# Gated linear attention and two expert layers on one core: prologue reordered, passes outermost, GpSimd's two-input steps on VectorE

## The chip, the cores and the metric

The kernel runs on one core of one Trainium2 chip. The metric is device microseconds (us) of one execution, the median of three runs. The engines are named as in the profile: PE is TensorE's matmuls and PEld its weight loads, DVE is VectorE, ACT is ScalarE, POOL is GpSimd, SP is SyncE, which issues most of the DMAs here.

## What is computed

Three parts follow each other; the output of each is the input of the next.

```python
f = 1 / (1 + exp(-f_logit))                      # attention: 4 batches, 8 heads, 768 steps, head size 48
for t in range(S):
    state = f[t][:, None] * state + outer(k[t], v[t])
    y[t] = q[t] @ state
x = y as [3072, 384]
p = domain_probs / (domain_probs.sum(-1) + 1e-9)  # mixture: 4 experts, 384 -> 1024 -> 384
x = sum over e of p[:, e] * (max(x @ w1[e], 0) @ w2[e])
out = ((x @ u1) * (x @ u2)) @ u3 @ uo             # last layer: 384 -> 1024 -> 1024 -> 384
```

All arrays are float32; the last layer's weights u1, u2, u3 and uo arrive as 64-bit floats.

## The kernel before, in words

**Precision.** The large products run in a form in which an operand is split into a high half (a copy rounded to the matmul's type, `fp32r`, by ScalarE) and a low half (the original minus the high half). Each product is three matmuls, or passes: high by high, high by low, low by high. `PASSES` (line 22) lists them as pairs (weight half, hidden half).

**Attention** goes in 24 chunks of 128 steps. Each chunk m is a list of steps: `a_exp`, `a_add`, `a_scan` (the running product of the gates, line 242), `a_ln`, `a_rec` (its reciprocal), `a_k` (keys times the running product, line 259), `a_t` (line 265), `a_q1` and `a_q2` (queries, lines 272 and 277), `a_p` (products of keys and queries on PE, the mask on DVE), `a_st` and `a_y` (the output, PE), `a_s` (the state, line 403), then `a_xh` and `a_xl` or `a_x` and `a_d`, which split the output into the halves of x. After each block of four chunks `attn_n` (line 427) sums x, for a check of range at the end.

**The mixture** (units of kind "E") goes in three super-blocks of two blocks of 512 tokens. A block of one expert is eight units f, one for each 128 hidden columns. The first block of the first expert is cut in two of 256 tokens, so its units are half as long. A unit has two parts. `stage1` (line 706): nine matmuls into one PSUM bank, then ACT writes the high half of the hidden tile with a ReLU (L727) and DVE the low half (L728). `stage2` (line 740): nine matmuls into three banks y0 to y2, for the three thirds of the output; the loop over the thirds is outermost, that over the passes inside. After the eighth unit DVE multiplies each bank by the gate (L774, or L771 for the first expert) and POOL adds it to the accumulator (L775).

**The last layer** (kind "M") has eight blocks of 384 tokens and 27 matmuls of 384 columns a unit. Its weights are first decoded from 64 bits by nine small steps a job (`decode_a`, `decode_b`, lines 543 and 559: seven on DVE, then one on ACT, then the product L572 on POOL), 16 jobs for u1 and u2 and 30 for uo and u3; the 30 are split into halves (`hilo_c`, line 609, low half on POOL) and multiplied ahead (`w3_mm`).

**Weights** come in chunks of 128x768. `feed` (line 841), called at the head of each unit, loads chunks ahead and splits at most one: high half on ACT (L174), low half on POOL (L175). Ten split chunks are held; a chunk is split when the oldest one's last unit is past. There are 160.

**The order** is written by hand: every engine runs its instructions in the order in which the program issues them. A prologue list `asteps` brings the first two chunks through and begins the third; `(warm, n)` are matmuls whose result is not used, `(feed_, 1)` splits a chunk, `gate_` normalises the experts' probabilities on DVE (line 129), `gate_rows_` transposes them on PE and sends them to memory, and `load_gate` (line 146) reads them back, spread over the partitions. The later steps have due times and `spread` (line 796) lays them over the units. The loop over the units issues, for unit i:

```python
feed(i, 1)
stage1(i)
if ends: stage2(i - 1)          # the unit before closed its block
...                             # first half of the steps planned here
if i and not ends: stage2(i - 1)
...                             # second half
```

## Time and profile before

| | us |
|---|---|
| median of 3 runs | 1290.7 (1290.09 to 1291.15) |
| the profiled execution | 1291.08 |
| its span, first to last instruction | 1289.4 |
| PE busy | 1260.7 (98%) |
| DVE busy | 634.9 (49%) |
| POOL busy | 531.0 (41%) |
| ACT busy | 427.7 (33%) |

The mean granted clock of PE is 0.993 of full speed. A line such as L728 is line 728 of the kernel. In the profile an entry "A <- B" under waits says that A stood idle until B was done. In the table by stage a row gives the window in us, its length, then busy us and (x instructions) of PE, PEld, DVE, ACT and POOL, the clock that was granted to PE as a share of full speed, the share of the DMA engines and GB/s. Matmuls are pipelined, so the time of a group of nine is read from start to start.

### The profile page before, as it was taken

The numbers are of one execution on the slowest core, as the hardware profiler recorded it, in microseconds if no ns is written. First come the engines' busy times: TensorE is split into PE (matmuls) and PEld (weight loads), VectorE is DVE, ScalarE is ACT, GpSimd is POOL, SyncE is SP. The second block draws the span as 40 slices with busy tenths as digits, with TensorE's granted clock in tenths as the row PEclk, the third lists the DMA queues.
The fourth block names the chain that finished last, engine by engine and source line by source line (L and its number), as shares of the span: only waits on it lengthen the run. The fifth ranks groups of instructions, "written<-read, shape, count | busy, mean of one in ns | idle before, by whom it ended". The sixth has DMA issues, their size and how long they took to land.

```text
span 1289.4 us, 18213 instructions
## 1 busy us (share of the span) xinstructions
PE 1260.7 (98%) x6935; PEld 1092.9 (85%) x6935; DVE 634.9 (49%) x1035; ACT 427.7 (33%) x760; POOL 531.0 (41%) x413
## 2 busy tenths in 40 slices
PE   7889999999999999999999999999999999999997
PEld 7888888888878888787888778788888999999997
DVE  7654443334465546565336766756624242332422
ACT  5434233342332323232222323324223433443431
POOL 3656345553542516354352635635433222222310
PEclk8989999999999999999999999999999999999999
DMA  7644343542635434252224422414134133231301
GB/s 197 181 146 121 98 133 101 148 125 72 170 115 134 140 105 148 81 156 82 77 80 134 121 80 87 144 56 131 55 99 129 56 94 98 91 104 55 117 1 40
DMA packets 107263, 138.74 MB, mean 108 GB/s; under 512 B 9664, under 2 KB 80672, under 8 KB 107168
## 3 DMA queue, kind: packets, MB, share of 16 engines
q1 hardware_dynamic: 106400, 137.16, 35.9%
q8 instruction: 56, 0.92, 0.3%
q10 hardware_dynamic: 768, 0.34, 0.1%
q14 instruction: 39, 0.32, 0.1%
HBM read 115.39 MB, written 14.20 MB: 101 GB/s over the span
## 4 chain that ended last, share of the span: by engine, by line
PE 88%; DVE 6%; POOL 2%; issue 2%; ACT 1%; DVEq 0%; ACTq 0%; POOLq 0%
PE hps L721 43%; PE y L755 36%; PE wps L634 3%; PE ps L319 2%; PE psy L359 2%; PE psy L343 1%; PE warm L469 1%; POOL w L175 1%; POOL acc L775 1%; PE psu L369 1%; DVE hid L728 1%; DVE dexp L553 1%; DVE pi L268 1%; DVE dexp L552 1%; PE psk L311 1%
## 5 line engine op out<-in xcount | busy, mean ns | idle before, releaser
L721 PE MATMUL hps<-x,w 128*128 128x512 f32 (+2 forms) x2952 | 648.3, 367 | 1.6 <-DVE ab L735 1.3
L721 PEld LDWEIGHTS hps<-x,w 128*128 128x128 f32 x2952 | 532.3, 189 | 75.8 <-DVE ab L735 1.6
L755 PE MATMUL y<-hid,w 128*128 128x512 f32 (+1 forms) x1800 | 443.7, 390 | 11.5 <-DVE hid L728 8.3
L175 POOL TENSOR_TENSOR w<-raw,w 128x768 fp32r<-128x768 f32 x160 | 302.9, 1895 | 293.0 <-ACT w L174 258.5
L755 PEld LDWEIGHTS y<-hid,w 128*128 128x128 f32 x1800 | 327.8, 189 | 88.8 <-DVE hid L728 12.0
L728 DVE SCALAR_TENSOR_TENSOR hid<-hps,hid 128x512 fp32r<-128x512 f32 (+1 forms) x200 | 133.6, 668 | 385.7 <-ACT hid L727 385.6
L727 ACT ACTIVATE hid<-hps 128x512 fp32r<-128x512 f32 (+1 forms) x200 | 115.6, 578 | 392.6 <-PE hps L721 392.5
L174 ACT ACTIVATE w<-raw 128x768 fp32r<-128x768 f32 x160 | 133.8, 837 | 55.2 <-PE y L755 55.2
L735 DVE TENSOR_TENSOR ab<-hps,a 128x384 f32<-128x384 f32 x64 | 35.6, 557 | 164.0 <-PE hps L721 164.0
L572 POOL TENSOR_TENSOR dman<-dman,dexp 128x384 f32<-128x384 f32 (+1 forms) x46 | 46.2, 1004 | 166.5 <-ACT dman L570 142.1
L755 PE MATMUL y<-w,hid 128*128 128x384 f32 x576 | 110.7, 337 | 0.1
L775 POOL TENSOR_TENSOR acc<-acc,tmp 128x512 f32<-128x512 f32 x54 | 71.9, 1361 | 79.0 <-DVE tmp L774 79.0
L755 PEld LDWEIGHTS y<-w,hid 128*128 128x128 f32 x576 | 100.7, 188 | 0.5 <-DVE hid L737 0.4
L570 ACT ACTIVATE dman<-dman 128x384 f32<-128x384 f32 (+1 forms) x46 | 24.0, 521 | 153.8 <-DVE dman L569 149.0
L736 ACT ACTIVATE hid<-ab 128x384 fp32r<-128x384 f32 x64 | 33.7, 526 | 115.3 <-DVE ab L735 115.3
L734 ACT ACTIVATE a<-hps 128x384 f32<-128x384 f32 x64 | 31.5, 492 | 77.5 <-PE hps L721 76.8
L737 DVE TENSOR_TENSOR hid<-ab,hid 128x384 fp32r<-128x384 f32 x64 | 35.8, 559 | 37.9 <-ACT hid L736 37.9
L414 POOL TENSOR_TENSOR state<-us,pwe 112x384 f32<-112x384 f32 x20 | 17.4, 869 | 88.3 <-DVE us L413 72.6
L774 DVE TENSOR_TENSOR tmp<-y,pb 128x512 f32<-128x512 f32 x54 | 35.5, 684 | 14.7 <-POOL acc L775 14.7
L268 DVE SCALAR_TENSOR_TENSOR pi<-pi,r 112x512 f32<-112x512 f32 (+1 forms) x26 | 33.7, 1295 | 14.8 <-POOL pends L263 13.0
L634 PE MATMUL wps<-uoh,u 128*128 128x384 f32 x192 | 38.0, 339 | 1.4 <-POOL u L620 0.9
L245 DVE TENSOR_TENSOR_SCAN pi<-ft,capt 112x516 f32<-112x516 f32 (+1 forms) x26 | 35.7, 1378 | 4.2 <-ACT ft L238 3.9
(87 smaller groups left out, 829.6 us busy)
## 6 DMA issues: line engine op xcount, KB each, us to landing
raw<-in_w_dram SPq DMA_DIRECT2D x112, 384.0 KB, 4.1
raw<-in_u_dram SPq DMA_DIRECT2D x27, 384.0 KB, 3.6
vt<-in_vp_dram SPq DMA_DIRECT2D x24, 288.0 KB, 4.2
pb<-pdr SPq DMA_DIRECT2D x24, 256.0 KB, 4.7
raw<-u1d SPq DMA_DIRECT2D x16, 384.0 KB, 3.2
raw<-u2d SPq DMA_DIRECT2D x16, 384.0 KB, 3.3
raw<-wdr SPq DMA_DIRECT2D x16, 384.0 KB, 3.4
x<-yr SPq DMA_DIRECT2D x80, 72.0 KB, 2.8
```

Source lines behind the costliest of these rows:

```text
L174: nc.scalar.activation(out=w[:, 0], in_=raw, func=AF.Copy)
L175: nc.gpsimd.tensor_tensor(out=w[:, 1], in0=raw, in1=w[:, 0].bitcast(F32), op=ALU.subtract)
L245: nc.vector.tensor_tensor_scan(out=pi.rearrange("p n t -> p (n t)"), data0=gates_of(m, g).rearrange("p n t -> p (n t)"), data1=capt[:, g[0 ...
L268: nc.vector.scalar_tensor_tensor(out=pi, in0=pi, scalar=-1.0, in1=r, op0=ALU.mult, op1=ALU.mult)
L572: nc.gpsimd.tensor_tensor(out=out, in0=s, in1=t.bitcast(F32), op=ALU.mult)
L634: nc.tensor.matmul(wps[ft], lhsT=w[:, a, i * 128:(i + 1) * 128], rhs=uoh[g // (NF // 2)][:, g % (NF // 2), b], start=(g == 0 and n == 0), ...
L721: nc.tensor.matmul(ps, lhsT=w[:, wl, j, fs], rhs=x[:, xl, j, t0:t1], start=(n == 0), stop=(n == 3 * KD - 1))
L727: nc.scalar.activation(out=h[:, 0], in_=prods[0], func=AF.Relu)
L728: nc.vector.scalar_tensor_tensor(out=h[:, 1], in0=prods[0], scalar=0.0, in1=h[:, 0].bitcast(F32), op0=ALU.max, op1=ALU.subtract)
L737: nc.vector.tensor_tensor(out=h[:, 1], in0=ab, in1=h[:, 0].bitcast(F32), op=ALU.subtract)
L755: nc.tensor.matmul(yps[t], lhsT=lhsT, rhs=rhs, start=(f == f0 and n == 0), stop=(f == f1 and n == 2))
L775: nc.gpsimd.tensor_tensor(out=at_, in0=at_, in1=tmp, op=ALU.add)
```

## The change

1. All operations of two inputs that POOL did, but for the first two splits and the 8-column product of `a_q2` (L285), go to DVE: the low halves of the weight chunks, `a_k`, `a_q1`, the state in `a_s`, the decode's product, its low halves, and the accumulation after each block.
2. In `stage2` the loop over the passes becomes the outer one, in the order high-high, low weight by high hidden, high weight by low hidden. In the last unit of a block the thirds stay outermost, with the passes in the new order.
3. In the prologue chunk 1's halves of x come before chunk 2's scan; the gate follows the state; its transpose, its two DMAs and the first `load_gate` move behind the first unit.
4. The sum of x over a block is three sums of 512 columns instead of one of 1536.

```diff
@@ -87,7 +87,7 @@
     pends = const.tile([RP, NCH, NP], F32, name="pends")
     pw = const.tile([RP, 3, NP], F32, name="pw")
     pwe = const.tile([RP, 3, NP, 2], F32, name="pwe")
-    xsum = const.tile([128, NBLK], F32, name="xsum")
+    xsum = const.tile([128, NBLK * KD], F32, name="xsum")
     state = const.tile([RP, NP, 128], F32, name="state")
     ft = const.tile([RP, 2, NP, 1 + C], F32, name="ft")
     wdr = dram.tile([FF, DM], F32, name="wdr")
@@ -172,7 +172,8 @@
         raw = raw_q.pop(c)
         w = wp.tile([128, 2, 768], F32R, tag="w", name="w")
         nc.scalar.activation(out=w[:, 0], in_=raw, func=AF.Copy)
-        nc.gpsimd.tensor_tensor(out=w[:, 1], in0=raw, in1=w[:, 0].bitcast(F32), op=ALU.subtract)
+        eng = nc.vector if len(wts) >= 2 else nc.gpsimd
+        eng.tensor_tensor(out=w[:, 1], in0=raw, in1=w[:, 0].bitcast(F32), op=ALU.subtract)
         wts[key] = w
 
 
@@ -258,7 +259,7 @@
 
     def a_k(m, g=ALL):
         pi, k = part(m, "pi", None, g), kq_of(m, 0, g)
-        eng = nc.vector if m < 3 else nc.gpsimd
+        eng = nc.vector
         eng.tensor_tensor(out=k, in0=k, in1=pi[:, :, 1:], op=ALU.mult)
         nc.gpsimd.tensor_copy(out=pends[:, m, g[0]:g[1]].unsqueeze(2), in_=pi[:, :, C:])
 
@@ -271,7 +272,7 @@
 
     def a_q1(m, g=ALL):
         r, q = part(m, "r", None, g), kq_of(m, 1, g)
-        eng = nc.vector if m < 3 else nc.gpsimd
+        eng = nc.vector
         eng.tensor_tensor(out=q, in0=q, in1=r, op=ALU.mult)
 
     def a_q2(m, g=ALL):
@@ -411,7 +412,7 @@
             nc.vector.tensor_copy(out=us, in_=u2)
         else:
             nc.vector.tensor_tensor(out=us, in0=u2, in1=state_of(m), op=ALU.add)
-        nc.gpsimd.tensor_tensor(
+        nc.vector.tensor_tensor(
             out=state_of(m + 1), in0=us, in1=pwe[:, m % 3].unsqueeze(3).to_broadcast([RP, NP, 2, D]), op=ALU.mult
         )
 
@@ -425,9 +426,11 @@
             eng.dma_start(out=x[R + d0:R + d0 + r1 - r0, :, j].bitcast(F32), in_=yr[r0:r1, :, KD].bitcast(F32))
 
     def attn_n(b):
-        nc.vector.tensor_reduce(
-            out=xsum[:, b:b + 1], in_=xt[b][:, 0].bitcast(F32).rearrange("p j t -> p (j t)"), axis=AX.X, op=ALU.add
-        )
+        for j in range(KD):
+            i = b * KD + j
+            nc.vector.tensor_reduce(
+                out=xsum[:, i:i + 1], in_=xt[b][:, 0, j].bitcast(F32), axis=AX.X, op=ALU.add
+            )
 
     def attn_done(m):
         if m % CB == CB - 1:
@@ -445,11 +448,11 @@
             out=mx[0:RP, 0:1], in_=pends.rearrange("p m n -> p (m n)"), axis=AX.X, op=ALU.max
         )
         nc.vector.tensor_scalar(out=ok[0:RP, 0:1], in0=mx[0:RP, 0:1], scalar1=LIM, scalar2=None, op0=ALU.is_le)
-        ex = const.tile([128, NBLK], I32, name="ex")
+        ex = const.tile([128, NBLK * KD], I32, name="ex")
         nc.vector.tensor_scalar(
             out=ex, in0=xsum.bitcast(I32), scalar1=0x7F800000, scalar2=None, op0=ALU.bitwise_and
         )
-        fin = const.tile([128, NBLK], F32, name="fin")
+        fin = const.tile([128, NBLK * KD], F32, name="fin")
         nc.vector.tensor_scalar(out=fin, in0=ex, scalar1=float(0x72000000), scalar2=None, op0=ALU.is_lt)
         nc.vector.tensor_reduce(out=ok[:, 1:2], in_=fin, axis=AX.X, op=ALU.min)
         verdict.append(ok)
@@ -488,9 +491,9 @@
         (a_scan, 1, G0), (a_scan, 1, G1), (a_p, 0), (a_ln, 1, G0), (a_rec, 1, G0), (a_ln, 1, G1), (a_rec, 1, G1),
         (load_f, 1), (load_kq, 1), (load_v, 2), (warm, 5), (a_y, 0), (a_k, 1, G0), (a_t, 1, G0), (a_q1, 1, G0),
         (a_q2, 1, G0), (a_k, 1, G1), (a_t, 1, G1), (a_q1, 1, G1), (a_q2, 1, G1), (a_xh, 0), (a_s, 0), (warm, 5),
-        (a_p, 1), (a_st, 1), (feed_, 1), (a_xl, 0), (warm, 3), (a_y, 1), (a_exp, 2), (a_add, 2), (feed_, 1), (a_scan, 2),
-        (gate_,), (a_xh, 1), (a_xl, 1), (gate_rows_,), (a_ln, 2), (a_rec, 2), (a_s, 1), (warm, 5), (a_k, 2), (a_t, 2), (a_q1, 2),
-        (a_q2, 2), (feed_, 1),
+        (a_p, 1), (a_st, 1), (feed_, 1), (a_xl, 0), (warm, 3), (a_y, 1), (a_exp, 2), (a_add, 2),
+        (feed_, 1), (a_xh, 1), (a_xl, 1), (warm, 8), (a_scan, 2), (a_ln, 2), (a_rec, 2), (a_s, 1), (gate_,), (a_k, 2),
+        (a_t, 2), (a_q1, 2), (a_q2, 2), (feed_, 1),
     ]
 
     def ahead(m):
@@ -569,7 +572,7 @@
         nc.vector.scalar_tensor_tensor(out=s, in0=l, scalar=2.0**-24, in1=g, op0=ALU.mult, op1=ALU.add)
         nc.scalar.activation(out=s, in_=s, func=AF.Identity, scale=2.0**-20, bias=1.0)
         out = s if out is None else out
-        nc.gpsimd.tensor_tensor(out=out, in0=s, in1=t.bitcast(F32), op=ALU.mult)
+        nc.vector.tensor_tensor(out=out, in0=s, in1=t.bitcast(F32), op=ALU.mult)
         return out
 
     u1i, u2i, u3i, uoi = (u.bitcast(I32) for u in (u1, u2, u3, uo))
@@ -616,7 +619,7 @@
                 uoh.append(xp.tile([128, NF // 2, 2, DM], F32R, tag=f"x{2 + j}", name="uoh"))
             w = uoh[j][:, g]
         nc.scalar.activation(out=w[:, 0], in_=s, func=AF.Copy)
-        eng = nc.gpsimd
+        eng = nc.vector
         eng.tensor_tensor(out=w[:, 1], in0=s, in1=w[:, 0].bitcast(F32), op=ALU.subtract)
         if key[0] == "3":
             u3v[key[1]] = w
@@ -746,15 +749,17 @@
         w = w.rearrange("p l (i c) -> p l i c", i=2)[:, :, f % 2, :]
         f0 = 0 if kind == "E" else e * NF // 2
         f1 = NF - 1 if kind == "E" else (e + 1) * NF // 2 - 1
-        for t in range(3):
-            if f == f0:
+
+        passes = list(enumerate(((0, 0), (1, 0), (0, 1))))
+        order = [(t, n, p) for n, p in passes for t in range(3)]
+        if f == f1:
+            order = [(t, n, p) for t in range(3) for n, p in passes]
+        for t, n, (wl, hl) in order:
+            if f == f0 and n == 0:
                 yps[t] = ps_y.tile([128, 512], F32, tag=f"y{t}", name="y")[:, 0:nt]
             ts = slice(t * 128, (t + 1) * 128)
-            for n, (wl, hl) in enumerate(PASSES):
-                lhsT, rhs = (w[:, wl, ts], h[:, hl]) if kind == "E" else (h[:, hl, ts], w[:, wl])
-                nc.tensor.matmul(
-                    yps[t], lhsT=lhsT, rhs=rhs, start=(f == f0 and n == 0), stop=(f == f1 and n == 2)
-                )
+            lhsT, rhs = (w[:, wl, ts], h[:, hl]) if kind == "E" else (h[:, hl, ts], w[:, wl])
+            nc.tensor.matmul(yps[t], lhsT=lhsT, rhs=rhs, start=(f == f0 and n == 0), stop=(f == f1 and n == 2))
         if f != f1:
             return
         fresh = (kind, hb, t0) not in begun
@@ -772,7 +777,7 @@
                 else:
                     tmp = two.tile([128, TB], F32, tag="tmp", name="tmp")[:, 0:nt]
                     nc.vector.tensor_tensor(out=tmp, in0=yps[t], in1=pe, op=ALU.mult)
-                    nc.gpsimd.tensor_tensor(out=at_, in0=at_, in1=tmp, op=ALU.add)
+                    nc.vector.tensor_tensor(out=at_, in0=at_, in1=tmp, op=ALU.add)
             if e == E - 1:
                 nc.sync.dma_start(out=x2d[:, :, hb * TB:(hb + 1) * TB], in_=a)
         else:
@@ -868,8 +873,10 @@
         warm(24)
         for st in asteps[:PRO]:
             run(st)
-        load_gate(0, 0)
         for i, u in enumerate(units):
+            if i == 1:
+                gate_rows_()
+                load_gate(0, 0)
             feed(i, 1)
             while any(c not in wts for c in unit_chunks(u)):
                 feed(i, 1)
```

## Rows read from the trace of the kernel before

**Rows 1.** The page: busy us of each engine, share, instructions

```profile
PE 1260.7 (98%) x6935; PEld 1092.9 (85%) x6935; DVE 634.9 (49%) x1035; ACT 427.7 (33%) x760; POOL 531.0 (41%) x413
```

**Rows 2.** Table by stage: window, busy PE, PEld, DVE, ACT, POOL, clock, DMA

```profile
0.00:29.04 29.04, 22.38 (x198) 21.32 (x198) 20.43 (x51) 15.11 (x33) 10.42 (x22) 0.92 0.78 197
29.04:62.63 33.59, 29.89 (x258) 28.18 (x257) 21.62 (x31) 16.31 (x34) 21.81 (x18) 0.92 0.60 178
62.63:91.66 29.03, 24.74 (x207) 23.61 (x205) 18.51 (x25) 10.69 (x20) 16.84 (x12) 0.88 0.57 167
91.66:690.00 598.34, 595.98 (x3284) 483.86 (x3283) 289.89 (x459) 184.90 (x304) 268.24 (x214) 1.00 0.41 118
690.00:905.00 215.00, 211.61 (x942) 173.91 (x941) 151.27 (x238) 68.43 (x123) 106.71 (x83) 1.00 0.33 100
905.00:1284.00 379.00, 376.06 (x2059) 361.99 (x2057) 133.23 (x235) 132.25 (x249) 106.99 (x65) 1.00 0.25 78
```

**Rows 3.** Waits of PE by line: us in total, times, longest us

```profile
PE y L755 <- DVE hid L728: 8.3, 8, 4.0
...
PE pT L139 <- DVE us L413: 4.5, 1, 4.5
...
PE y L755 <- ACT hid L727: 2.9, 3, 2.0
```

**Rows 4.** Timeline, 47 to 88 us: start, length, engine, line, operation

```profile
48.09 2.80 DVE L240 TENSOR_SCALAR ft<-ft 112x512 f32<-112x512 f32 x1
...
74.19 3.62 POOL L175 TENSOR_TENSOR w<-raw,w 128x768 fp32r<-128x768 f32 x2
...
74.25 1.24 PE L721 MATMUL hps<-x,w 128*128 128x256 f32 x9
...
74.27 7.11 DVE L268 SCALAR_TENSOR_TENSOR pi<-pi,r 112x512 f32<-112x512 f32 x1
...
79.02 1.81 POOL L175 TENSOR_TENSOR w<-raw,w 128x768 fp32r<-128x768 f32 x1
...
83.43 2.08 PE L755 MATMUL y<-hid,w 128*128 128x256 f32 x8 [4.02 <-DVE hid L728]
...
85.30 2.12 PE L721 MATMUL hps<-x,w 128*128 128x256 f32 x9
```

**Rows 5.** Timeline, prologue, steps of VectorE

```profile
19.53 1.44 DVE L392 TENSOR_TENSOR x<-psy,x 96x384 fp32r<-96x384 f32 x4
...
22.61 1.45 DVE L132 TENSOR_SCALAR psum__366<-psum__366 128x24 f32<-128x24 f32 x1
...
30.77 0.16 DVE L282 SCALAR_TENSOR_TENSOR pw<-pi,r 112x4 f32<-112x4 f32 x1
```

**Rows 6.** Groups by line and shape: count, busy us, mean ns, idle before

```profile
L175 POOL TENSOR_TENSOR w<-raw,w 128x768 fp32r<-128x768 f32 x160 | 302.9, 1895 | 293.0 <-ACT w L174 258.5 <-issue 18.5 <-PE hps L721 12.1
...
L262 POOL TENSOR_TENSOR kq<-kq,pi 112x512 f32<-112x512 f32 x21 | 25.2, 1198 | 0.0
...
L262 DVE TENSOR_TENSOR kq<-kq,pi 112x512 f32<-112x512 f32 x1 | 0.7, 683 | 0.0
...
L737 DVE TENSOR_TENSOR hid<-ab,hid 128x384 fp32r<-128x384 f32 x64 | 35.8, 559 | 37.9 <-ACT hid L736 37.9
...
L174 ACT ACTIVATE w<-raw 128x768 fp32r<-128x768 f32 x160 | 133.8, 837 | 55.2 <-PE y L755 55.2
```

**Rows 7.** Decode line L553: duration ns min/median/max, and its group

```profile
L553 DVE TENSOR_SCALAR dexp<-dexp x46: 229/361/1894, 357.2 to 931.9; 128x384 int32<-128x384 int32 x45, 128x128 int32<-128x128 int32 x1
...
L553 DVE TENSOR_SCALAR dexp<-dexp 128x384 int32<-128x384 int32 (+1 forms) x46 | 35.3, 767 | 1.6
```

**Rows 8.** Timeline at a block's end, 170 to 175 us

```profile
170.84 2.26 PE L755 MATMUL y<-hid,w 128*128 128x512 f32 x9
...
171.67 0.69 DVE L728 SCALAR_TENSOR_TENSOR hid<-hps,hid 128x512 fp32r<-128x512 f32 x1 [3.75 <-ACT hid L727]
...
172.94 2.25 PE L721 MATMUL hps<-x,w 128*128 128x512 f32 x9
```

## The prediction

> **What bounds the kernel now.** I read the engines' totals first. TensorE is busy for 98% of the span [rows 1], so a wait elsewhere only counts where TensorE stands still. The table by stage shows where it does [rows 2]: idle time is span minus PE busy. The prologue up to the first unit leaves 6.7 us, the stretch to 62.63 us 3.7, the one to 91.66 us 4.3; then 2.4 in 598 us, 3.4 in 215 and 2.9 in 379; the 5.4 us after 1284 are the drain. The granted clock is 0.92, 0.92 and 0.88 in the first three stretches and 1.00 after. Between the levels 1.2 and 2.4 GHz, 0.92 means 16% of the time at the lower one, and a busy microsecond there does half the work: 33.59 x 0.16 / 2 = 2.7 us lost in the second stretch, 29.03 x 0.24 / 2 = 3.5 in the third. So 3.7 + 2.7 + 4.3 + 3.5 = 14.2 us is all that lies between 29 and 92 us, and under 9 us in the 1190 that follow.
>
> The waits name the causes [rows 3]: the low half of the hidden tile (VectorE, L728) for 8.3 us, the gate's transpose 4.5, the high half (ScalarE, L727) 2.9. The timeline shows what is behind the longest [rows 4]. The VectorE step L268, whose 512 columns should take some 0.7 us (683 ns is another such step [rows 6]), runs for 7.11 us from 74.27, as long as GpSimd has two-input work in its queue: two splits, a third operation, one more split that ends at 80.83. L728 is queued behind it and TensorE stops for 4.02 us. The nine matmuls of 256 columns then take 2.12 us instead of 1.24. At 48.09 the same happens to L240, 2.80 us.
>
> A page of the Trainium skill, SBUF — State Buffer, section Who interferes with whom, has a rule for it: VectorE operations with two SBUF inputs or in a two-port mode exclude a GpSimd operation that reads SBUF, and the loser blocks for that one instruction. By that rule the stall should have ended with one split, some 2 us, and removing it would be worth some 2.5 us less. The rows show L268 held through four GpSimd operations, and they are what I use.
>
> **The change part by part.** *GpSimd operations to VectorE.* Moved are 158 of the 160 splits (L175), 54 accumulations (L775: three in each of the 18 blocks that add to an earlier expert's result), 42 key and query products (21 each, the row of L262 stands for both), and 46 decode products, 30 low halves, 20 state products of 384 columns (counts without a row from the loops). VectorE's prices: 683 ns for 512 columns and 559 ns for 384, so 0.97 ns a column, and 683 + 256 x 0.97 = 931 ns for 768 [rows 6]. The sum is 158 x 0.93 + 96 x 0.68 + 96 x 0.56 = 266 us. VectorE rises from 635 to at most 901 us, 70% of the span. Against this stands what GpSimd costs it today: L553 has a median of 361 ns, a mean of 767 and a maximum of 1894 [rows 7]. TensorE is the cover: from 91.66 to 905 it is idle 5.8 us in all. New are two waits inside VectorE's queue: a split now waits there for ScalarE's high half, a decode product for ScalarE's step before it. Queued behind both are L728, which TensorE wants, and the attention steps, for which ScalarE waits in turn; the slack below is what covers them.
>
> *The early stretches.* With GpSimd nearly empty (8-column products and copies stay), L268, L240 and the scans go back to their uncontended time, and the key product no longer waits behind 1.9 us splits. In the queue at 74 us VectorE now has, between two L728, one split 0.93, L268 0.69 and the sum of x (three pieces of some 0.6 instead of one of 1.7: no difference); the next L728 is due about 4 us after 73.8, and TensorE wants it at 79.4. That stall goes whole, with its slow matmuls. The stalls before 62 us hang on the same chain, but there VectorE also gets some ten splits, so I take 4 of 6.4 there and 6 of 7.8 after: **-10 us**. The ends are 0 (the splits take the place of the waits) and -14.2.
>
> *Prologue.* Until chunk 2's query is ready (end of L282, 30.9) TensorE cannot go past its first unit's nine matmuls [rows 5]. VectorE ends chunk 0's low part at 20.97. Before, the scan, the gate (2.3 us, 1.45 of it L132 beside a GpSimd split) and chunk 1's low part followed. Now: wait for ScalarE until about 22.4, low part 1.5, scan 1.2, two state steps 1.1, gate 1.0 to 2.3, four steps of 0.69 and 0.16, which ends at 30.1 to 31.4. The first unit starts earlier, but the next attention matmuls wait for that. The transpose's wait of 4.5 goes; what is late next is this chain. I take **-1 us**, between -2 and +0.5. The gate's rows and their two DMAs come one unit later on SP, behind that unit's loads; the first reader is the accumulation after 62 us, over 20 us later: nothing, unless that cover shrinks under the few microseconds a load takes.
>
> *Passes outermost.* The low half of the hidden tile is wanted at the seventh of nine matmuls instead of the second: about 1.2 us more slack per unit at 0.233 us each ((172.94 - 170.84)/9) [rows 8]. Where a block begins, all three banks are now wanted within three matmuls instead of seven, and VectorE empties them with two operations each. At a block's end L728 ends at 172.36, and six steps of 0.68 follow; the fifth, which frees the third bank, ends at 175.8. TensorE comes back at 172.94 + 2.10 = 175.04 and wants that bank at 175.5. So 0.3 us at a block's end, more with other VectorE work ahead, nothing where attention matmuls lie between. There are 18 such ends: 0 to 18 x 0.5 = 9, against up to 5.8 of old idle that may go. I take **+3 us** (-4 to +9). Alternating banks I cost at nothing: the nine matmuls of L721 write one bank, those of L755 three, and both take 2.10.
>
> *Last stage.* Its splits go to VectorE, where the stage has much room (133 us of 379); the last unit's first two passes no longer wait for the low half: **-0.3 us**.
>
> The profiled execution took 1291.08 us, 0.4 above the median. 1291.1 - 1 - 10 + 3 - 0.3 = 1282.8, and **1282.4** against the median.
>
> **The rivals.** *A: VectorE's queue becomes the bound (slower).* In 690 to 905 VectorE is busy 151 us; GpSimd's 107 become 53 to 61 at the ratios 0.93/1.90 and 0.68/1.20; the sum is 208 of 215. If three lines of a decode job each give back 0.41 (767 mean less 361 median [rows 7]), 30 jobs return 37 us: 80 to 97% full. In order, it also stands still while ScalarE makes the high half of a split (837 ns). Were one split and its hold, 1.8 us, ahead of the six steps at each of the 18 ends, each would cost 2.1: 1290.7 - 11.3 + 38 = 1317, and 1298 with half of them. It decides from 11.3/18 = 0.6 us per end. Against it: the hold only arises when VectorE is not behind, and the low half has 1.2 us more slack. The Trainium skill, Perfetto Trace Analysis, section Optimizing Scalar/DVE Operations, advises to hand work to GpSimd when VectorE is saturated, and adds that it may not help since the two share a port. By the advice this change goes the wrong way in that stretch; no row here shows VectorE saturated.
>
> *B: the early stalls come back in another coat.* L728 waits behind splits that wait for ScalarE, and the early gain is 3 instead of 11: 1290.7 - 3 + 3 = about 1290.
>
> *C: alternating banks costs.* The starts can hide 0.01 us in two bank changes; six more in some 230 units would be 7 us: 1289. Nothing in L721 against L755 speaks for it.
>
> That the change does not do what it says I see only in small print: the 8-column L285 products stay on GpSimd, as do the copies, and move none of these sums.
>
> **How the numbers follow.** Forecast 0.75, A 0.13, B 0.07, C 0.05. A measurement of this kernel can tell 0.2%, 2.6 us, from no change. The forecast's own range, 1275 to 1288, is all faster (beyond that lie the rivals); B and C fall within 2.6 us; A is slower: 0.75, 0.12, 0.13. The low end is 1291 - 2 - 14 = 1275 with nothing given back; the high end, 1296, takes in B, C and the mild part of A, and leaves out the rest of A and a little below.
>
> **What would show it.** Right: L268 and L240 with no value above 1 us; no TensorE wait over 1 us between 62 and 92 us and a clock near 1.00 there; the 512-column block stream reached near 81 instead of 91.66 us; GpSimd under 30 us; VectorE near 800. Wrong: waits of L755 for L774 or L775's results at block ends beyond 10 us in sum; TensorE idle growing in 690 to 905; ScalarE's L727 waiting on VectorE chains; or an unchanged start of the 512-column stream.

## The result, and the profile after

The kernel after takes **1277.79 us** (median of 4 runs, 1277.05 to 1278.3) against 1290.93 of the kernel before in the same session; the ratio is **0.9898, with an interval of 0.9884 to 0.9912**. It is 13.1 us faster; 8.3 were predicted, within a range of 1275 to 1296. The profiled execution took 1278.3 us with a span of 1276.6, so it lies 0.5 above the median.

The engines' totals of the page of after, in the columns of [rows 1]:

```profile
PE 1256.9 (98%) x6941; PEld 1088.6 (85%) x6941; DVE 787.9 (62%) x1397; ACT 429.3 (34%) x760; POOL 27.1 (2%) x63
```

GpSimd fell from 531 to 27 us, VectorE rose by only 153: the moved operations run about twice as fast there (a split takes 955 ns on average, 1895 before [rows 6]), and what VectorE had lost beside GpSimd came back. Line numbers have shifted: the hidden tile's matmuls are L724, its halves L730 and L731, the output's matmuls L762, the low half of a split L176, the block end's two steps L779 and L780.

The table by stage of after, in the columns of [rows 2]: four stretches whose ends are the same points of the work (first unit, second token block of the first expert, first unit of 512 columns, first unit of the last layer), a fixed one, and two inside the second:

```profile
0.00:23.96 23.96, 21.56 (x202) 20.10 (x203) 15.43 (x43) 13.48 (x29) 7.47 (x19) 1.00 0.97 240
23.96:60.32 36.36, 29.97 (x260) 27.90 (x259) 29.70 (x54) 18.15 (x37) 2.69 (x6) 0.91 0.57 164
60.32:82.43 22.11, 21.84 (x207) 20.92 (x205) 19.74 (x37) 10.70 (x20) 1.61 (x2) 1.00 0.77 219
82.43:964.58 882.15, 879.25 (x4542) 717.02 (x4541) 588.37 (x1039) 275.48 (x463) 15.28 (x36) 1.00 0.39 112
690.00:905.00 215.00, 213.33 (x958) 177.40 (x957) 162.88 (x326) 70.08 (x124) 0.00 (x0) 1.00 0.34 100
24.00:37.00 13.00, 8.03 (x54) 7.42 (x54) 12.04 (x22) 6.08 (x11) 1.91 (x2) 0.74 0.32 112
31.00:36.00 5.00, 5.00 (x31) 4.78 (x32) 4.52 (x7) 1.39 (x3) 1.70 (x1) 0.50 0.04 10
```

The stretch that took 29.03 us at a clock of 0.88 [rows 2] takes 22.11 at 1.00, with 0.3 us of idle TensorE. The one from 82.43 to 964.58 is the stream of 512 columns; in the kernel before it is 91.66 to 976.74, whose line shows 5.75 us idle (885.08 less 879.33) where after has 2.90:

```profile
91.66:976.74 885.08, 879.33 (x4543) 717.09 (x4541) 471.01 (x746) 274.35 (x463) 403.71 (x319) 1.00 0.38 111
```

Counted by these points, the gain lies at 9.23 us before the stream (91.66 to 82.43), 2.93 in the stream (885.08 to 882.15) and 1.03 in the last layer (302.04 to 301.01, first unit to the start of the last group of output matmuls); the drain gives 0.4 back. That is the 12.8 us between the spans.

The waits of PE by line in after (us in total, times, longest), and of PEld the largest:

```profile
PE psk L312 <- issue: 3.4, 1, 3.4
...
PE y L762 <- ACT hid L730: 1.8, 2, 1.0
PE wps L637 <- DVE u L623: 1.7, 2, 1.5
PE ps L320 <- DVE kq L280: 1.5, 1, 1.5
...
PE hps L724 <- DVE ab L738: 0.2, 1, 0.2
```

```profile
PEld y L762 <- DVE tmp L779: 4.3, 9, 0.5
```

The 8.3 us for the low half of the hidden tile [rows 3] are gone: L731 is in no row. What is new is a wait behind the first unit (L312 and L320, 4.9 us in one place; "issue" means that the profile shows nothing that was waited for), where the kernel before had 4.5 us for the gate's transpose [rows 3], and, on the weight loads alone, a wait for the block end's L779. The third cause is small: PE waited 1.3 us in the last layer for L735 before, and 0.2 for the same step, L738, after; that accounts for its 1.03.

The lines of VectorE that GpSimd used to hold, in after (duration ns as min/median/max):

```profile
L269 DVE SCALAR_TENSOR_TENSOR pi<-pi,r x26: 420/686/695, 7.5 to 640.7; 112x512 f32<-112x512 f32 x22, 112x256 f32<-112x256 f32 x4
...
L241 DVE TENSOR_SCALAR ft<-ft x20: 417/418/422, 49.6 to 616.6; 112x512 f32<-112x512 f32 x20
...
L556 DVE TENSOR_SCALAR dexp<-dexp x46: 227/360/363, 349.0 to 918.8; 128x384 int32<-128x384 int32 x45, 128x128 int32<-128x128 int32 x1
```

L268's 7.11 us and L240's 2.80 [rows 4] have become 0.70 and 0.42 at most, and the decode line, which had a maximum of 1894 ns [rows 7], ends at 363. In the timeline of after, the place that stopped TensorE for 4.02 us [rows 4]:

```profile
71.52 0.42 DVE L731 SCALAR_TENSOR_TENSOR hid<-hps,hid 128x256 fp32r<-128x256 f32 x1
...
71.86 0.68 DVE L269 SCALAR_TENSOR_TENSOR pi<-pi,r 112x512 f32<-112x512 f32 x1
...
72.46 1.87 DVE L431 TENSOR_REDUCE xsum<-x 128x1 f32<-128x512 f32 x3
...
74.24 0.95 DVE L176 TENSOR_TENSOR w<-raw,w 128x768 fp32r<-128x768 f32 x1
...
75.10 0.42 DVE L731 SCALAR_TENSOR_TENSOR hid<-hps,hid 128x256 fp32r<-128x256 f32 x1
...
76.78 1.23 PE L762 MATMUL y<-hid,w 128*128 128x256 f32 x9
```

Between two L731 stand one L269, the three sums and one split, as forecast; the low half is done at 75.52, 1.26 us before the matmuls that read it start.

### The profile page after: what moved, and what is told of

It reads as the page before. It is cut to its first block, busy times and chain, and to the rows that moved or that the text cites. A ratio compares the mean times of both kernels' runs of the same rounds, so it can differ in the third digit from the quotient of the medians.

```text
span 1276.6 us, 17977 instructions
## 1 busy us (share of the span) xinstructions
PE 1256.9 (98%) x6941; PEld 1088.6 (85%) x6941; DVE 787.9 (62%) x1397; ACT 429.3 (34%) x760; POOL 27.1 (2%) x63
## 4 chain that ended last, share of the span: by engine, by line
PE 91%; DVE 4%; DMA 2%; ACT 1%; issue 1%; SPq 0%; DVEq 0%; ACTq 0%
PE hps L724 45%; PE y L762 38%; PE wps L637 2%; PE ps L320 2%; PE psy L360 2%; DMA raw<-in_w_dram 1%; PE psy L344 1%; DVE tmp L779 1%; DVE acc L780 1%; PE psu L370 1%; DMA ft<-in_fkq_dram 1%; PE psk L312 0%; DVE hid L731 0%; ACT hid L730 0%; DVE pi L246 0%
## 5 line engine op out<-in xcount | busy, mean ns | idle before, releaser
L724 PE MATMUL hps<-x,w 128*128 128x512 f32 (+2 forms) x2952 | 647.3, 366 | 0.5 <-DVE x L393 0.3
L724 PEld LDWEIGHTS hps<-x,w 128*128 128x128 f32 x2952 | 531.5, 188 | 74.6 <-DVE ab L738 0.5
L762 PE MATMUL y<-hid,w 128*128 128x512 f32 (+1 forms) x1800 | 442.1, 389 | 2.2 <-ACT hid L730 1.8
L762 PEld LDWEIGHTS y<-hid,w 128*128 128x128 f32 x1800 | 326.3, 188 | 79.3 <-DVE tmp L779 4.3
L731 DVE SCALAR_TENSOR_TENSOR hid<-hps,hid 128x512 fp32r<-128x512 f32 (+1 forms) x200 | 133.7, 668 | 225.3 <-ACT hid L730 224.8
L730 ACT ACTIVATE hid<-hps 128x512 fp32r<-128x512 f32 (+1 forms) x200 | 115.9, 579 | 409.4 <-PE hps L724 409.3
L176 DVE TENSOR_TENSOR w<-raw,w 128x768 fp32r<-128x768 f32 x158 | 150.9, 955 | 40.3 <-ACT w L174 39.6
L738 DVE TENSOR_TENSOR ab<-hps,a 128x384 f32<-128x384 f32 x64 | 35.7, 557 | 123.8 <-PE hps L724 123.8
L762 PE MATMUL y<-w,hid 128*128 128x384 f32 x576 | 110.6, 337 | 0.0
L762 PEld LDWEIGHTS y<-w,hid 128*128 128x128 f32 x576 | 100.6, 188 | 0.3 <-DVE hid L740 0.3
L575 DVE TENSOR_TENSOR dman<-dman,dexp 128x384 f32<-128x384 f32 (+1 forms) x46 | 25.4, 553 | 27.8 <-ACT dman L573 27.8
L780 DVE TENSOR_TENSOR acc<-acc,tmp 128x512 f32<-128x512 f32 x54 | 37.4, 692 | 1.9
L637 PEld LDWEIGHTS wps<-uoh,u 128*128 128x128 f32 x192 | 34.3, 188 | 4.1 <-DVE u L623 2.3
L779 DVE TENSOR_TENSOR tmp<-y,pb 128x512 f32<-128x512 f32 x54 | 36.9, 683 | 0.0
L323 DVE TENSOR_TENSOR asb<-ps,cmask 128x512 f32<-128x512 f32 x48 | 30.8, 683 | 4.6 <-PE ps L320 3.8
L246 DVE TENSOR_TENSOR_SCAN pi<-ft,capt 112x516 f32<-112x516 f32 (+1 forms) x26 | 29.7, 1144 | 4.1 <-ACT ft L239 3.8
```

Of the source, the lines that this page charges most:

```text
L176: eng.tensor_tensor(out=w[:, 1], in0=raw, in1=w[:, 0].bitcast(F32), op=ALU.subtract)
L637: nc.tensor.matmul(wps[ft], lhsT=w[:, a, i * 128:(i + 1) * 128], rhs=uoh[g // (NF // 2)][:, g % (NF // 2), b], start=(g == 0 and n == 0), ...
L724: nc.tensor.matmul(ps, lhsT=w[:, wl, j, fs], rhs=x[:, xl, j, t0:t1], start=(n == 0), stop=(n == 3 * KD - 1))
L730: nc.scalar.activation(out=h[:, 0], in_=prods[0], func=AF.Relu)
L731: nc.vector.scalar_tensor_tensor(out=h[:, 1], in0=prods[0], scalar=0.0, in1=h[:, 0].bitcast(F32), op0=ALU.max, op1=ALU.subtract)
L738: nc.vector.tensor_tensor(out=ab, in0=prods[1], in1=a, op=ALU.mult)
```

## The experiments

The theory tested first: the gain is GpSimd's two-input work leaving VectorE's way, nearly all of it ahead of the stream, and prologue and passes are worth little either way. Its rivals: the new prologue or the new order of the passes makes a good part of the gain; the splits alone make it; VectorE, now fuller, gives part of it back. Each kernel was timed in 3 rounds beside the kernel before (1291.01, 1290.46 and 1290.70 us in the three sessions). A diff is against the kernel after unless the text says otherwise. The intervals take in the spread of the kernel before; between kernels of the study the single runs are the finer measure, and where a difference to after is claimed below, the runs of the two don't overlap.

**engines_only: the kernel before with part 1 of the change alone** (the seven engine choices; old prologue, passes and sum).

```diff
-        nc.gpsimd.tensor_tensor(out=w[:, 1], in0=raw, in1=w[:, 0].bitcast(F32), op=ALU.subtract)
+        eng = nc.vector if len(wts) >= 2 else nc.gpsimd
+        eng.tensor_tensor(out=w[:, 1], in0=raw, in1=w[:, 0].bitcast(F32), op=ALU.subtract)
...
-        eng = nc.vector if m < 3 else nc.gpsimd
+        eng = nc.vector
...
-                    nc.gpsimd.tensor_tensor(out=at_, in0=at_, in1=tmp, op=ALU.add)
+                    nc.vector.tensor_tensor(out=at_, in0=at_, in1=tmp, op=ALU.add)
```

> The kernel before with one part of the change alone: the two-input GpSimd operations go to VectorE (the first two splits stay), prologue, order of the passes and sum of x as before. Theory (freeing the queue that VectorE shares something with is most of the gain): 1278 to 1283, L268 never above 1 us, the first 512-column matmuls at 82 to 85 us. Rival (the order of the passes carries it): 1286 to 1291, with waits for the low half of the hidden tile at 15 us or more, since VectorE is now fuller and the low half is still wanted at the second matmul. Rival (the prologue carries it): 1286 to 1290.

Measured: **1277.24 us, ratio 0.9895 (0.9879 to 0.9912)**, the whole gain, and 0.8 us below the range that was expected. Its stream starts at 79.97 us, 2.5 us ahead of the kernel after and earlier than the 82 to 85 expected, and takes 883.89. So the other parts together are worth nothing, and the next runs show that they are worth something each, with opposite signs.

**undo_splits: the splits back on GpSimd, all else as after.**

```diff
-        eng = nc.vector if len(wts) >= 2 else nc.gpsimd
-        eng.tensor_tensor(out=w[:, 1], in0=raw, in1=w[:, 0].bitcast(F32), op=ALU.subtract)
+        nc.gpsimd.tensor_tensor(out=w[:, 1], in0=raw, in1=w[:, 0].bitcast(F32), op=ALU.subtract)
```

> The changed kernel with the 158 weight splits back on GpSimd, everything else changed. Theory (what costs is GpSimd's two-input work beside VectorE's, and the splits are 303 of its 531 us): 1282 to 1288, with VectorE steps of two inputs again stretched to 3 us or more in the first 90 us and a TensorE wait of over 1 us there. Rival (GpSimd's slowness in attention's and the decode's own chain is what cost): 1276 to 1279, no change or slightly better, because VectorE is 150 us emptier.

Measured: **1285.15 us, 0.9954 (0.9938 to 0.9971)**. It loses 7.4 us, but not where that was looked for: the stream starts at 82.44 us, as in the kernel after (82.43). Its timeline at the place of the old stall:

```profile
71.23 5.90 POOL L175 TENSOR_TENSOR w<-raw,w 128x768 fp32r<-128x768 f32 x3
```

```profile
71.83 1.81 DVE L268 SCALAR_TENSOR_TENSOR pi<-pi,r 112x512 f32<-112x512 f32 x1
```

Three splits run back to back on GpSimd, yet L268 is done after 1.81 us, while the second of them still runs, and TensorE does not stop. The loss is in the stream, which takes 888.46 us where after takes 882.15. A block's end in this kernel's timeline, 276 to 288 us:

```profile
280.53 0.69 DVE L779 TENSOR_TENSOR acc<-acc,tmp 128x512 f32<-128x512 f32 x1
...
281.59 1.83 POOL L175 TENSOR_TENSOR w<-raw,w 128x768 fp32r<-128x768 f32 x1 [3.48 <-ACT w L174]
...
281.85 2.12 DVE L779 TENSOR_TENSOR acc<-acc,tmp 128x512 f32<-128x512 f32 x1
...
283.90 0.68 DVE L778 TENSOR_TENSOR tmp<-y,pb 128x512 f32<-128x512 f32 x1
...
284.63 1.90 PE L761 MATMUL y<-hid,w 128*128 128x512 f32 x7 [1.51 <-DVE tmp L778]
```

The accumulation (here L779), which GpSimd did itself before, now stands in VectorE's queue between the steps that empty the banks. A split on GpSimd holds it for 2.12 us instead of 0.69, the third bank comes free late, and TensorE waits 1.51 us. The waits of PE and PEld in this kernel's stream, by line, have these rows at the top:

```profile
PE y L761 <- DVE tmp L778: 4.5, 3, 1.5
```

```profile
PEld y L761 <- DVE tmp L778: 8.9, 10, 1.9
```

**undo_others: only the splits on VectorE;** key and query products, state, decode's product and low halves, and accumulation back on GpSimd.

```diff
-        eng = nc.vector
+        eng = nc.vector if m < 3 else nc.gpsimd
...
-        nc.vector.tensor_tensor(out=out, in0=s, in1=t.bitcast(F32), op=ALU.mult)
+        nc.gpsimd.tensor_tensor(out=out, in0=s, in1=t.bitcast(F32), op=ALU.mult)
...
-                    nc.vector.tensor_tensor(out=at_, in0=at_, in1=tmp, op=ALU.add)
+                    nc.gpsimd.tensor_tensor(out=at_, in0=at_, in1=tmp, op=ALU.add)
```

> The changed kernel with only the splits on VectorE; the key and query products, the state, the decode's products and low halves and the accumulations are back on GpSimd. Theory: a smaller loss than with the splits back, 1279 to 1283, since these are 228 us of GpSimd's work and seldom queue up behind each other. Rival (their own chains cost): 1283 to 1288.

Measured: **1274.04 us, 0.9869 (0.9853 to 0.9886)**, 3.7 us better than the kernel after. The expectation missed the sign: beyond the splits, the moves cost. Its stream starts at 82.16 us and takes 879.15, 3.0 less than after's; PE's waits in it are down to two lines:

```profile
PE y L762 <- ACT hid L730: 1.0, 2, 0.7
PE wps L637 <- POOL u L623: 0.9, 1, 0.9
```

**undo_passes: the old order of the passes in stage2.**

```diff
-        order = [(t, n, p) for n, p in passes for t in range(3)]
-        if f == f1:
-            order = [(t, n, p) for t in range(3) for n, p in passes]
-        for t, n, (wl, hl) in order:
...
+        for t in range(3):
...
+            for n, (wl, hl) in enumerate(PASSES):
```

> The changed kernel with the loop over the thirds of the output outermost again and the old order of the passes. Theory: 1277 to 1281; the waits of TensorE for the low half rise by 1 to 3 us, and the weight loads' waits for the banks at a block's begin (4.3 us) go. Rival (the order of the passes is what lets VectorE carry the load): 1284 or more.

Measured: **1280.57 us, 0.9923 (0.9907 to 0.9940)**, 2.8 us slower than after: the new order gains. The waits of PE by line that after doesn't have:

```profile
PE y L758 <- DVE hid L731: 3.1, 5, 0.7
```

**passes_only and prologue_only: the kernel before with part 2 alone, and with part 3 alone** (the same hunks as in the change, so the diffs are not repeated).

> The kernel before with the new order of the passes alone. Theory: 1287 to 1290; some of the 8.3 us of waits for the low half go (the third-pass slack is about 1.2 us a unit), the 4 us stall only by the 0.6 us that five more short matmuls cover. Rival (this part carries the gain): 1283 or less.

> The kernel before with the new prologue alone. Theory: 1289 to 1292. Rival: 1286 or less.

Measured: passes_only **1287.45 us, 0.9976 (0.9966 to 0.9986)**; the passes gain 3.0 us without the engine moves as well. prologue_only **1291.26 us, 1.0003 (0.9993 to 1.0012)**: no difference. In both, L268 still has a maximum of 7.1 us and the stream starts at 89.95 and 89.96 us (the trace of prologue_only is of an execution of 1289.56, 1.7 below its median). With undo_splits (82.44) and undo_others (82.16) that shows one thing: beside the new prologue and passes, taking either half of the two-input work off GpSimd, the splits or the rest, removes the early stall. Prologue or passes alone do not; the two together, with all the work left on GpSimd, were not run.

**undo_prologue: the old prologue, all else as after.**

```diff
-        (feed_, 1), (a_xh, 1), (a_xl, 1), (warm, 8), (a_scan, 2), (a_ln, 2), (a_rec, 2), (a_s, 1), (gate_,), (a_k, 2),
-        (a_t, 2), (a_q1, 2), (a_q2, 2), (feed_, 1),
+        (feed_, 1), (a_scan, 2),
+        (gate_,), (a_xh, 1), (a_xl, 1), (gate_rows_,), (a_ln, 2), (a_rec, 2), (a_s, 1), (warm, 5), (a_k, 2), (a_t, 2), (a_q1, 2),
+        (a_q2, 2), (feed_, 1),
...
+        load_gate(0, 0)
...
-            if i == 1:
-                gate_rows_()
-                load_gate(0, 0)
```

> The changed kernel with the prologue as before (scan, gate, then chunk 1's halves; the gate's rows and the first load of gates ahead of the first unit). Theory: 1277 to 1280, as the chain to chunk 2's query ends within 1 us of the same time either way. Rival (the prologue is worth 4 us or more, the 4.5 us that TensorE waited for the gate's transpose): 1282 or more.

Measured: **1275.32 us, 0.9881 (0.9864 to 0.9897)**, 2.5 us faster than after in the medians and below the 1277 to 1280 expected; its stream starts at 80.66 us, 1.8 earlier. Once GpSimd is out of the way, the new prologue costs. TensorE in the timeline of after:

```profile
23.96 1.37 PE L724 MATMUL hps<-x,w 128*128 128x256 f32 x9
...
28.77 0.58 PE L312 MATMUL psk<-ident,kq 112*128 112x112 f32 x4 [3.44 <-issue]
...
30.88 2.08 PE L320 MATMUL ps<-kq 48*128 48x128 f32 x16 [1.53 <-DVE kq L280]
...
32.99 2.27 PE L724 MATMUL hps<-x,w 128*128 128x256 f32 x9
...
35.05 1.74 PE L762 MATMUL y<-hid,w 128*128 128x256 f32 x9
36.64 0.63 PE L724 MATMUL hps<-x,w 128*128 128x256 f32 x4
```

and of undo_prologue:

```profile
27.06 0.45 PE L139 MATMUL pT<-ident,praw 128*96 128x128 f32 x1 [4.27 <-DVE us L414]
27.30 2.34 PE L472 MATMUL warm<-cmask,ident 128*128 128x128 f32 x10
29.30 1.64 PE L724 MATMUL hps<-x,w 128*128 128x256 f32 x9
...
31.25 1.16 PE L320 MATMUL ps<-kq 48*128 48x128 f32 x16
32.35 1.33 PE L724 MATMUL hps<-x,w 128*128 128x256 f32 x9
33.52 1.23 PE L762 MATMUL y<-hid,w 128*128 128x256 f32 x9
34.58 1.24 PE L724 MATMUL hps<-x,w 128*128 128x256 f32 x9
```

After starts its first unit 5.3 us earlier and is 2.1 us behind by the third group of L724 (36.64 against 34.58). All of that is lost behind the query. Its products (L320) start 0.37 us earlier in after (30.88 against 31.25), but from there to the third group it takes 5.76 us instead of 3.33: 2.01 instead of 1.10 for the 16 products, 2.06 and 1.59 instead of 1.17 and 1.06 for the two groups of nine, and 0.10 for the gate's transpose, which now stands between them. In after the granted clock is 0.50 from 31 to 36 us (the last line of the table by stage), just there. In undo_prologue it falls as well, but from 27 to 30 us, where TensorE runs unused matmuls (L472) and begins its first unit; over 24 to 37 us it is 0.74 in after and 0.87 here:

```profile
24.00:37.00 13.00, 9.94 (x79) 9.68 (x80) 11.68 (x22) 6.15 (x12) 2.28 (x4) 0.87 0.57 172
27.00:30.00 3.00, 2.94 (x14) 2.94 (x15) 2.08 (x5) 2.42 (x5) 0.00 (x0) 0.50 0.28 73
```

**undo_xsum: one sum of 1536 columns instead of three.**

```diff
-        for j in range(KD):
-            i = b * KD + j
...
+        nc.vector.tensor_reduce(
+            out=xsum[:, b:b + 1], in_=xt[b][:, 0].bitcast(F32).rearrange("p j t -> p (j t)"), axis=AX.X, op=ALU.add
+        )
```

> The changed kernel with one sum of 1536 columns instead of three of 512. Theory: within 0.5 us of the changed kernel, 1277.3 to 1278.3, as both occupy VectorE for some 1.8 us in a row. Rival (a single long operation delays the low half): 1279 or more.

Measured: **1277.77 us, 0.9897 (0.9880 to 0.9913)**: no difference.

**acc_pool: only the accumulation back on GpSimd.**

```diff
-                    nc.vector.tensor_tensor(out=at_, in0=at_, in1=tmp, op=ALU.add)
+                    nc.gpsimd.tensor_tensor(out=at_, in0=at_, in1=tmp, op=ALU.add)
```

> The changed kernel with the 54 accumulations alone back on GpSimd. Theory (they stand between VectorE's steps that free the three banks, so that the next block's weight loads wait, 4.3 us in the changed kernel): that wait goes, 1274.5 to 1276. Rival (with only the splits on VectorE the gain came from the decode's products and low halves, or from the whole load): 1277 to 1278.5.

Measured: **1276.16 us, 0.9889 (0.9873 to 0.9906)**, 1.6 us below after and 0.2 above the range that the theory gave; the stream takes 880.37 us instead of 882.15, and the rows of L762 waiting for L779 are gone. That is the price of the third bank (below), and under half of the 3.7 us that separate undo_others from after.

**warm_gap: unused matmuls into the prologue's gap, the gate behind chunk 2's query.**

```diff
-        (feed_, 1), (a_xh, 1), (a_xl, 1), (warm, 8), (a_scan, 2), (a_ln, 2), (a_rec, 2), (a_s, 1), (gate_,), (a_k, 2),
-        (a_t, 2), (a_q1, 2), (a_q2, 2), (feed_, 1),
+        (feed_, 1), (a_xh, 1), (a_xl, 1), (warm, 20), (a_scan, 2), (a_ln, 2), (a_rec, 2), (a_s, 1), (a_k, 2),
+        (a_t, 2), (a_q1, 2), (a_q2, 2), (gate_,), (feed_, 1),
```

> The changed kernel with 12 more unused matmuls ahead of the first unit and the gate's four steps behind chunk 2's query. Theory (the new prologue lost some 2.5 us because TensorE stood still from 25 to 31 us, and the next matmuls ran at the lower clock): the query's products start some 0.9 us earlier and at the upper clock, the first 512-column matmuls at 79 to 80 instead of 82.4, 1274 to 1276. Rival (it is the order of VectorE's steps that costs, not the clock): 1277 to 1278.

Measured: **1275.90 us, 0.9885 (0.9869 to 0.9902)**, 1.9 us below after; the stream starts at 80.90 us and not at 79 to 80. Both the theory and its rival have a part in it. With the gate's steps out of the way the products of L320 start at 30.17 us, 0.7 earlier than in after; they now run at the upper clock, and the next group starts 1.21 us behind them instead of 2.11, which gives 0.9. But the clock still fell: from 31.38 us two groups take 2.07 and 2.03 us.

**best: undo_others and warm_gap together.** Only the splits on VectorE, the new passes, and warm_gap's prologue.

> Only the splits on VectorE, the new order of the passes, and the prologue of the run before with more unused matmuls: the two gains add, 1270 to 1272. Rival (with keys and queries back on GpSimd the shorter start is eaten by contention): 1273 to 1274.

Measured: **1271.55 us, 0.9857 (0.9841 to 0.9874)**, 6.2 us below the kernel after and 19 below the one before in its session. Its stream starts at 79.49 us and takes 879.13; over the whole execution VectorE is busy 728.0 us and GpSimd 251.0.

## Why the prediction was right, and where not

The forecast fell 4.8 us short of the gain. Two of its terms had the wrong sign: the prologue came out 3.9 us worse than its term and the passes 5.8 better. That most of this cancels is luck. The rest is 1.7 us from the early stretches, 1.2 from the stream and 0.7 from the last stage, less 0.4 for the drain. The starts of the second token block and of the stream tell the early terms apart: 62.63 and 91.66 us in the kernel before, 57.83 and 79.97 in engines_only, 60.74 and 82.87 in undo_passes (engines and prologue), 60.32 and 82.43 in after.

- **Early stretches, -10: right, and somewhat small.** engines_only gains 4.8 us up to the second block (62.63 to 57.83) and 6.9 behind it (29.03 to 22.14; 6 forecast): -11.7. Of the 4.8, 1.3 lie ahead of the first unit (it starts at 27.75 instead of 29.04), where this term had nothing; the stretch behind it gains 3.5 (33.59 to 30.08; 4 forecast). The mechanism is shown: L268 and L240 back at their short durations, no TensorE wait over 1 us between 62 and 92, the clock at 1.00 there, all as the signs asked for. The stream start near 81 us came at 82.43, for the next term's sake.
- **Prologue, -1: the term that failed, by 3 to 4 us.** Between engines_only and undo_passes, which differ by the prologue and the sum of x, it costs 2.9 us (79.97 to 82.87); undo_prologue gives 1.8 in the trace and 2.5 in the medians. The step that failed is "what is late next is this chain". The chain came as priced: it ends at 30.90 us (L283, 30.75 plus 0.15), inside the 30.1 to 31.4 forecast and no earlier than the 30.93 of before [rows 5], as chunk 1's low part waits for ScalarE until 23.05 and not 22.4. What I left out is the clock at which TensorE runs behind it: the products of the query and the next two groups take 2.3 us more than the same work in undo_prologue, at a granted clock of 0.50, and that is the whole loss. after, undo_passes and prologue_only, with the new order, all have the clock at 0.50 from 31 to 36 us; undo_prologue and engines_only, with the old one, have it there from 27 to 30, ahead of the query. Idle time alone does not tell the two orders apart: TensorE idles 3.44 and 1.53 us in the new and 4.27 in the old, so why the clock falls when it does is not shown. On the kernel before, where the old order had its own 4.5 us wait [rows 3], the same edit costs nothing.
- **Passes outermost, +3: wrong in sign.** It gains 2.8 us (undo_passes) or 3.0 (passes_only). I named both sides, 0 to 9 us of bank waits against up to 5.8 of old idle, and took the wrong one as the larger. The bank wait is there and has the size forecast: in after, at the block end of 278 us, the nine matmuls behind it take 2.43 us from start to start instead of 2.10, the 0.3 of the prediction.

```profile
282.35 0.69 DVE L779 TENSOR_TENSOR tmp<-y,pb 128x512 f32<-128x512 f32 x1
...
282.38 2.60 PE L762 MATMUL y<-hid,w 128*128 128x512 f32 x9
...
283.09 1.45 PEld L762 LDWEIGHTS y<-hid,w 128*128 128x128 f32 x7 [0.52 <-DVE tmp L779]
...
284.81 1.55 PE L724 MATMUL hps<-x,w 128*128 128x512 f32 x6
```

 But it occurs at 9 places and not 18, never above 0.5 us, and acc_pool puts the whole of it at 1.6 to 1.8. What goes is larger: in the stream of undo_passes the weight loads of the output's matmuls wait 3.8 us for L731 and 2.3 for L730, in after not at all and 1.4. The sign that I had set for failure, over 10 us of such waits, was far off.
- **GpSimd to VectorE in the stream, costed at nothing: right for all of them together, wrong for their parts.** The stream gains 1.2 us in engines_only (885.08 to 883.89). But splits alone would have gained more: with the rest left on GpSimd it takes 879.15 instead of 882.15 (undo_others against after). 1.8 of those 3.0 us belong to the accumulation. The other 1.2 stay open: one candidate, the decode's low half, shows in PE's wait for L623 (1.7 us in after, 0.9 in undo_others), and no run moves it alone. VectorE's total, "near 800", was 788; a split, priced at 931 ns, took 955:

```profile
L176 DVE TENSOR_TENSOR w<-raw,w 128x768 fp32r<-128x768 f32 x158 | 150.9, 955 | 40.3 <-ACT w L174 39.6
```

- **Last stage, -0.3:** it was -1.03, and for another reason than the one given. At the layer's begin three VectorE steps (L685, at 984.45 us) took 4.70 us beside GpSimd's accumulations and a split; in after (L688) they take 1.49, and TensorE waits 0.2 us instead of 1.3 for the step queued behind them.
- **The sum of x and the drain:** nothing, as costed; the drain took 0.4 more.

**Rival A**, VectorE's queue as the bound, did not happen: in 690 to 905 us it is busy 162.88 of 215, 76%, below the 80 to 97 forecast, and TensorE's idle time there falls from 3.4 us to 1.7. Added work of 53 to 61 us returned 41 to 49 (151 plus those, less 163), more than the 37 allowed, because every step of the decode came back to its median. Its hold is real, though: VectorE stands still 82 times for ScalarE's high half, at most 2.1 us. **B** is excluded by the timeline; **C** by undo_passes, and directly: in after nine matmuls with the banks in turn take 2.10 us (278.20 to 280.30), as before. The Trainium skill, Perfetto Trace Analysis, section Optimizing Scalar/DVE Operations, says that offloading between VectorE and GpSimd might not help, as they share a read port. The runs agree and divide it: leaving the splits on GpSimd costs 7.4 us, leaving the rest there gains 3.7.

## What to carry to other kernels

Two engines that hold each other are not put right by emptying one. Move the long operations that come back to back, here the 768-column splits; leave short ones where they free another engine, above all between the steps that empty a bank TensorE wants next. Let the operand that is ready last be read by the last pass. And where a reorder moves TensorE's gap, look at which matmuls then run at the lower clock: here the old order spent it on unused ones, the new one on those that everything else waits for.

## What had not been expected of the hardware

**How long VectorE is held varies.** In the kernel before L268 is held through four GpSimd operations, 7.11 us [rows 4]; beside three splits in a row in undo_splits it is let in after one, 1.81. The Trainium skill, SBUF — State Buffer, section Who interferes with whom, has the loser block for one instruction: undo_splits agrees, the row of before does not, and none of these runs says what decides. The same section exempts VectorE operations with one SBUF input, as long as they do not run in a two-port mode. L728 has one (its other input is the PSUM bank), and the traces agree: its maximum is 694 ns before, 695 after. L240 has one too and was held, 2.80 us [rows 4]; the section counts `tensor_scalar`, which it is, among the operations that can enter such a mode, and no row shows whether it did.

**GpSimd loses too.** Its product of 8 columns, which stays there, took 223 ns on average before (L285, 22 times) and 467 after (L286). The median of all 26 is 204 in both; the longest went from 523 to 1717. What holds it are the splits: the average is 217 in undo_splits, where all but the splits are on VectorE, and 524 in undo_others, where only they are. The longest, in after, stands beside two splits in a row and ends 0.06 us after the second:

```profile
30.82 1.82 DVE L176 TENSOR_TENSOR w<-raw,w 128x768 fp32r<-128x768 f32 x2
...
30.98 1.72 POOL L286 TENSOR_TENSOR pwe<-pw,hm 112x8 f32<-112x8 f32 x1 [4.92 <-DVE pw L283]
```

**The clock was not the same for the same work.** warm_gap and best give TensorE the same operations in the same order from 22 to 35 us, with gaps of 1.52 and 1.57 us in the same place; in warm_gap two groups behind it ran at the lower clock, in best none did. The windows 24 to 37 us, first of warm_gap:

```profile
24.00:37.00 13.00, 11.47 (x93) 11.10 (x92) 12.29 (x23) 6.26 (x12) 0.53 (x3) 0.87 0.35 118
```

then of best:

```profile
24.00:37.00 13.00, 11.42 (x103) 10.73 (x102) 11.37 (x21) 6.59 (x12) 2.01 (x4) 1.00 0.44 149
```

0.87 and 1.00 of the upper level, 2.4 GHz, for one and the same order. From the start of the first of the two groups to the end of their stretch it is 3.74 us in warm_gap (31.38 to 35.12) and 2.40 in best (31.05 to 33.45), so in these two traces 1.3 us are the clock's. Executions of one and the same kernel differ as well: of the ten of prologue_only, four took 1289.5 to 1289.8 us at a mean clock of 0.994, six 1291.2 to 1291.9 at 0.991 to 0.993. What makes the clock fall in the one and not in the other stays open.
